# Attention and a squared-ReLU MLP on one core: the weights' sign on ScalarE, denominators on VectorE, and a new order of the work

## The chip, the cores and the metric

One core of a Trainium2 chip. The metric is the device time of one execution, in microseconds (us); smaller is better. Three runs of the kernel before took 637.91, 639.02 and 640.23 us, median 639.02.

## What is computed

q, k and v are 4 batches x 12 heads x 448 rows x 64, float32. The two weight matrices come in float64 (a float32 array times a NumPy float64 scalar), so the kernel has to turn 64-bit words into float32 itself.

```python
scores = cap * np.tanh(scale * np.matmul(q, k.transpose(0, 1, 3, 2)) / cap)
attn = np.exp(scores - np.max(scores, axis=-1, keepdims=True))
attn = attn / (np.sum(attn, axis=-1, keepdims=True) + 1e-09)
x = np.matmul(attn, v)               # 1792 tokens x 768
r = np.maximum(x @ w_in, 0.0)        # w_in 768 x 2048
out = (s * (r * r) + b) @ w_out      # w_out 2048 x 768
```

## The kernel before, in words

All work is recorded as small groups of instructions in a plan (class `Plan`). Each group has a rank, the tiles it reads and writes, and one or more engines that may do it. `emit` then runs a list scheduler over the groups: it keeps a clock per engine, takes the group that can start first (among ready ones that of the lowest rank, with a preference for the same kind of work on TensorE), books buffers, and issues the instructions in that order. Nothing is rearranged afterwards, so each engine runs its instructions strictly in the order that the scheduler's assumed times gave. The table `CHOICE` sets that order: an `at` entry (rank, step) per unit of work, the engines allowed per operation, and a few margins (`late`, `lag`, `cling`).

The units:

- `a` (batch, pair of head pairs): `load` brings K, Q and V; `scores` makes per 128 keys one TensorE product into a `ps_s` buffer (two of them), a tanh and an exp on ScalarE (L512, L516, L520). The last 64 keys of two head pairs share one chunk (the tail), which needs K and Q of both. `pv` multiplies by V and by ones into the single `ps_v` buffer in two parts (L570, L578), ScalarE copies it out (L598), and `normal` sends the sums through four small DMAs (L533), adds the two halves and the guard on GpSimd (L541, L542), takes reciprocals on VectorE (L545), and broadcasts them through DRAM (L547, L552).
- `w` (8 groups of w_in, three pieces each, `win`) and `o` (6 groups of w_out, four pieces each, `wout`): a piece is loaded as pairs of 32-bit words (`piece`, L654). In the 64-bit word the exponent has 11 bits; VectorE takes the low word down to 3 bits (L662), puts the sign in with a second pass (L663), an engine scales the high word, read as float32, by 2^-112 (L434 or L436), and VectorE shifts and joins the two (L666). For w_in the squares (L700 to L702) are summed on TensorE (the norm, L712), the largest goes through another small TensorE product that gives it to all lanes (L477), a chain of VectorE instructions of one column makes the scales (L728 to L733), and the weights are split in two float16 parts. For w_out the column sums of each group are formed by additions and one small product (L785).
- `m1` and `m2` (batch): the two MLP products, each in three float16 products (L843 to L845, L1094 to L1096). Batches 2 and 3 use a form with 7 in place of 8 block products (L1003), whose weights the units `p` prepare (`mix`).

The first two w_in groups have their pieces in the memory of `gt`, all others in a pool `w` of seven slots. All loads and stores are issued by SP, in the scheduler's order, and SP reuses eight DMA semaphores in turn.

Of the kernel before, what the change touches and what calls it, by code (L numbers as in the profile page):

```python
# [243 lines left out]
def arrange(units, at):  # L244

    key = {}
    for name, pre, _ in units:
# [5 lines left out]
    'bias': 1.806,  # L253
    'shy': {'DVE': 0.3, 'POOL': 0.5},
# [36 lines left out]
    'late': 0.621,  # L291
    'lag': 0.0,
    'cling': 19.274,
# [4 lines left out]
    'tail': 0.9,  # L298
    'evac': ('ACT',),
    'sq': ('ACT', 'DVE', 'POOL'),  # L300
    'expo': ('DVE', 'POOL'),
# [24 lines left out]
def attention_moe_kernel(  # L326
# [157 lines left out]
    def load(bb, c2, rank, vrank):  # L484
        if bb == c2 == 0:
            rank = -90
# [36 lines left out]
    def normal(bb, c2, rank):  # L523
# [15 lines left out]
        def whole():  # L539
            a = P[kc][:, 0]  # L540
            nc.gpsimd.tensor_tensor(a, a, P[kc][:, 1], ALU.add)  # L541
            nc.gpsimd.tensor_scalar(a, a, guard[:, 0:1], 0.0, ALU.add, ALU.add)  # L542

        gps(0.55, rank, whole, r=["guard", *((kc, h, i) for h in range(2) for i in range(2))], w=[kc], port=True)
        dve(0.32, rank, lambda: nc.vector.reciprocal(P[kc][:, 0], P[kc][:, 0]), w=[kc])  # L545
# [14 lines left out]
    def pv(bb, c2, rank, step):  # L560
# [54 lines left out]
        def gather():  # L615
# [6 lines left out]
            r=[("xm", bb, c) for c in range(NP)], w=[("xn", bb)], port=True,  # L622
# [24 lines left out]
    def piece(kr, src, n, rank, over=()):  # L647
# [13 lines left out]
        def sign():  # L661
            nc.vector.tensor_scalar(lo(), lo(), 29, None, ALU.logical_shift_right)  # L662
            nc.vector.scalar_tensor_tensor(lo(), hi(), -0x80000000, lo(), ALU.bitwise_and, ALU.bitwise_or)  # L663
# [508 lines left out]
    def put(name, pre, fn):  # L1172
        units.append((name, pre, fn))
# [18 lines left out]
    for d in range(ND):  # L1192
        put(("o", d), [("w", NG - 1)], lambda rank, step, d=d: wout(d, rank))
# [71 lines left out]
```

## Time and profile before

| | |
|---|---|
| median of three runs | 639.02 us |
| profiled execution | 639.61 us |
| its span (first to last instruction) | 637.8 us |
| TensorE (PE) busy | 627.0 us, 98% |
| VectorE (DVE) / ScalarE (ACT) / GpSimd (POOL) busy | 400.2 / 351.7 / 208.1 us |
| moved by DMA | 101.67 MB |

Busy TensorE time is taken from modelled ends of pipelined matmuls, so slow stretches hide in it: a matmul that runs at half the clock counts as busy. They are seen in the granted clock of a stretch and in the distance of instructions.

### The profile page before, as it was taken

To read this page: it belongs to the slowest core of one execution; us is meant where nothing else is said; L and a number is where in the kernel's file an instruction comes from. 1 tells how busy PE (TensorE), PEld (TensorE's weight loads), DVE (VectorE), ACT (ScalarE), POOL (GpSimd) and SP (SyncE) were. 2 spreads that over 40 slices of the span, in tenths; PEclk is the share of its full clock that TensorE was granted. 3 is DMA by queue.
4 is the path that set the end of the run, shared out by engine and by line. 5 is a ranking of instruction groups with operands and counts; after the bars stand their busy time and mean duration, and the time that the engine had idled before them with its cause. 6 is when DMAs were issued, how large, how long until landed. Compare 5 with 4: busy or idle time off the path is not lost.

```text
span 637.8 us, 11435 instructions
## 1 busy us (share of the span) xinstructions
PE 627.0 (98%) x4404; PEld 331.4 (52%) x4404; DVE 400.2 (63%) x810; ACT 351.7 (55%) x472; POOL 208.1 (33%) x238
## 2 busy tenths in 40 slices
PE   7999899999999999999999999999999999999997
PEld 2332344344444433434454445555558996556997
DVE  5986857888797878788773341577767222537322
ACT  5889787886884585684674531346354002445100
POOL 3343511546456544466151020117643000105000
PEclk9999899999999999999999999999999999999999
DMA  8766423654262775853854013385412774001671
GB/s 301 293 184 193 124 86 107 215 175 143 60 234 59 251 211 179 272 200 92 282 195 157 1 48 128 146 280 212 164 48 89 239 260 147 1 2 53 223 256 67
DMA packets 54774, 101.67 MB, mean 159 GB/s; under 512 B 16192, under 2 KB 34752, under 8 KB 54720
## 3 DMA queue, kind: packets, MB, share of 16 engines
q1 hardware_dynamic: 54720, 100.95, 48.2%
q8 instruction: 34, 0.56, 0.4%
q14 instruction: 20, 0.16, 0.1%
HBM read 82.58 MB, written 18.17 MB: 158 GB/s over the span
## 4 chain that ended last, share of the span: by engine, by line
PE 85%; DMA 8%; DVE 3%; ACT 1%; SPq 1%; POOL 1%; issue 0%; ACTq 0%
PE ps_v L570 9%; PE ps_m L1003 9%; PE ps_s L512 7%; PE ps_s L1003 6%; PE ps_m L843 6%; PE ps_s L844 6%; PE ps_m L844 6%; PE ps_s L843 6%; PE ps_m L845 6%; PE ps_s L845 6%; PE ps_m L1094 5%; PE ps_m L1095 5%; PE ps_m L1096 5%; PE ps_v L578 4%; DMA gt<-in_w_in 2%; DMA w<-in_w_out 2%
## 5 line engine op out<-in xcount | busy, mean ns | idle before, releaser
L1003 PEld LDWEIGHTS <-w 128*128 128x128 f16 x1008 | 96.6, 98 | 1.0
L516 ACT ACTIVATE bed<-ps_s,arena 128x896 f32<-128x896 f32 x84 | 81.5, 1006 | 9.9 <-PE ps_s L512 8.2
L520 ACT ACTIVATE bed<-bed,par 128x896 f32<-128x896 f32 x84 | 84.2, 1040 | 0.2
L570 PE MATMUL ps_v<-bed 128*32 128x448 f32 x768 | 83.0, 548 | 0.8 <-ACT pw L598 0.6
L512 PE MATMUL ps_s<-bed 64*128 64x448 f32 (+1 forms) x384 | 80.6, 578 | 1.9 <-DMA bed<-in_qT 1.6
L1094 PE MATMUL ps_m<-gt,w 128*128 128x448 f16 x192 | 67.7, 353 | 0.0
L843 PE MATMUL ps_m<-x,w 128*128 128x448 f16 x192 | 67.7, 353 | 0.0
L1096 PE MATMUL ps_m<-gt,w 128*128 128x448 f16 x192 | 67.7, 353 | 0.0
L844 PE MATMUL ps_s<-x,w 128*128 128x448 f16 x192 | 67.7, 353 | 0.0
L844 PE MATMUL ps_m<-x,w 128*128 128x448 f16 x192 | 67.7, 353 | 0.0
L845 PE MATMUL ps_m<-x,w 128*128 128x448 f16 x192 | 67.7, 353 | 0.0
L843 PE MATMUL ps_s<-x,w 128*128 128x448 f16 x192 | 67.7, 353 | 0.0
L1095 PE MATMUL ps_m<-gt,w 128*128 128x448 f16 x192 | 67.7, 352 | 0.0
L845 PE MATMUL ps_s<-x,w 128*128 128x448 f16 x192 | 67.7, 352 | 0.0
L843 PEld LDWEIGHTS <-w 128*128 128x128 f16 x384 | 37.5, 98 | 37.3 <-issue 2.1
L845 PEld LDWEIGHTS <-w 128*128 128x128 f16 x384 | 37.5, 98 | 35.0
L844 PEld LDWEIGHTS <-w 128*128 128x128 f16 x384 | 37.6, 98 | 33.8
L512 PEld LDWEIGHTS ps_s<-bed 64*128 64x128 f32 (+1 forms) x384 | 27.4, 177 | 43.5 <-issue 12.2
L938 ACT ACTIVATE pw<-ps_s,arena 128x448 f32<-128x448 f32 x32 | 20.1, 632 | 52.6 <-PE ps_s L845 49.7
L570 PEld LDWEIGHTS ps_v<-bed 128*32 128x32 f32 x768 | 20.3, 109 | 51.4 <-issue 35.7
L444 POOL TENSOR_TENSOR pw<-pw 128x224 f32<-128x224 f32 x24 | 21.6, 912 | 77.6 <-ACT pw L942 71.2
L578 PE MATMUL ps_v<-bed,ones 128*32 128x448 f32 x288 | 45.5, 545 | 0.0
(142 smaller groups left out, 1012.8 us busy)
## 6 DMA issues: line engine op xcount, KB each, us to landing
w<-w SPq DMA_DIRECT2D x48, 512.0 KB, 4.9
w<-in_w_out SPq DMA_DIRECT2D x24, 512.0 KB, 5.0
w<-ws SPq DMA_DIRECT2D x24, 512.0 KB, 4.9
w<-in_w_in SPq DMA_DIRECT2D x18, 512.0 KB, 5.5
bed<-in_v SPq DMA_DIRECT2D x24, 256.0 KB, 4.2
ws<-w SPq DMA_DIRECT2D x12, 512.0 KB, 2.9
bed<-in_kT SPq DMA_DIRECT2D x24, 224.0 KB, 3.3
bed<-in_qT SPq DMA_DIRECT2D x24, 224.0 KB, 3.6
```

Source lines behind the costliest of these rows:

```text
L512: nc.tensor.matmul(P[kp][o, h, 0:S], keys, P[q][rows], start=True, stop=True)
L516: 1.01, rank, lambda: nc.scalar.activation(P[kh], P[kp][:, :, 0:S], AF.Tanh, scale=tsc[:, 0:1]),
L520: 1.04, rank, lambda: nc.scalar.activation(P[kh], P[kh], AF.Exp, scale=par[:, 0:1]), r=["par"], w=[kh],
L570: nc.tensor.matmul(P[kp][o, 0, 0:S], P[kv][:, c, o], prob(c, h), start=(c == 0), stop=(c == NC))
L578: nc.tensor.matmul(P[kp][o, 1, 0:S], w, ph, start=first, stop=last)
L843: nc.tensor.matmul(ps[:, 0:S], wh, x[:, 0], start=(c == 0), stop=False)
L844: nc.tensor.matmul(ps[:, 0:S], wh, x[:, 1], start=False, stop=False)
L845: nc.tensor.matmul(ps[:, 0:S], wl, x[:, 0], start=False, stop=(c == NP - 1))
L1003: nc.tensor.matmul(at(), w(g, zw), b(g, zb), start=g == 0 and x == 0, stop=g == n - 1 and x == 2,)
L1094: nc.tensor.matmul(ps[:, 0:S], wh, ghi[:, f], start=(f == 0), stop=False)
L1095: nc.tensor.matmul(ps[:, 0:S], wh, glo[:, f], start=False, stop=False)
L1096: nc.tensor.matmul(ps[:, 0:S], wl, ghi[:, f], start=False, stop=(f == NF - 1))
```

## The change

Five edits, beside a new table of ranks.

1. In `piece`, the second sign pass is gone. The high word is scaled by one ScalarE instruction whose slope for negative inputs is 2^32 times that for positive ones, so that after the shift the sign stands in the right place; or, where the scheduler prefers VectorE, by two instructions. GpSimd no longer takes part.

```diff
-        def sign():
+        def low():
             nc.vector.tensor_scalar(lo(), lo(), 29, None, ALU.logical_shift_right)
-            nc.vector.scalar_tensor_tensor(lo(), hi(), -0x80000000, lo(), ALU.bitwise_and, ALU.bitwise_or)
...
-        scaled(CHOICE["expo"], n, rank, hf, hf, 2.0 ** -112, [(kr, "s")], [kr])
+        def two():
+            nc.vector.tensor_scalar(hf(), hf(), 2.0 ** -112, None, ALU.mult)
+            nc.vector.scalar_tensor_tensor(hf(), hf(), 2.0 ** 32, hf(), ALU.mult, ALU.min)
+        ways = {
+            "ACT": (
+                0.29 + n * 0.00084,
+                lambda: nc.scalar.activation(hf(), hf(), AF.Prelu, scale=2.0 ** -112, alpha=2.0 ** 32),
+            ),
+            "DVE": (0.36 + n * 0.00158, two),
+        }
```

2. In `normal`, the sum of the halves and the guard is one VectorE instruction, right before the reciprocal.

```diff
-            nc.gpsimd.tensor_tensor(a, a, P[kc][:, 1], ALU.add)
-            nc.gpsimd.tensor_scalar(a, a, guard[:, 0:1], 0.0, ALU.add, ALU.add)
+            nc.vector.scalar_tensor_tensor(a, a, guard[:, 0:1], P[kc][:, 1], ALU.add, ALU.add)
+            nc.vector.reciprocal(a, a)
```

3. In `win`, what depends on a lane's own maximum alone (`own`: root, reciprocal, square) becomes a group that may run while TensorE gives the maximum to all lanes; `fin` keeps the rest.

4. The first K, Q and cap loads get ranks far below all others (`rank = -9e12` and `-1e13` in place of -90 and -100), and `wout` may start only after all w_in groups in rank.

5. `CHOICE`: all ranks, `bias` 1.806 to 3.059, `late` 0.621 to 0.309, `lag` 0.0 to 0.452, `cling` 19.274 to 14.502, `expo` from VectorE and GpSimd to ScalarE and VectorE. For example:

```diff
-        ('w', 0): (58.5, 0.01), ('w', 1): (226.3, 0.01), ('w', 2): (-88.5, 0.01), ('w', 3): (581.8, 0.01),
+        ('w', 0): (255.1, 0.0), ('w', 1): (-84218287.2, 0.01), ('w', 2): (20.7, 0.0), ('w', 3): (256.7, 0.0),
```

How the order moves, at three places. First, SP and ScalarE at the start of the program, before the change (`bed` holds the attention tiles, `gt` and `w` the weight pieces):

```order
L1140 DMA par_130<-in_cap 128x1
L488 DMA bed_60<-in_kT 128x448
L490 DMA bed_60<-in_qT 128x448
L654 DMA w_155<-in_w_in 128x1024
L654 DMA w_157<-in_w_in 128x1024
L654 DMA w_159<-in_w_in 128x1024
L488 DMA bed_60<-in_kT 128x448
L490 DMA bed_60<-in_qT 128x448
```

```order
L1153 ACTIVATE arena_131<-par_130 128x1
L516 ACTIVATE bed_60<-ps_s_173,arena_131 128x896
L516 ACTIVATE bed_60<-ps_s_177,arena_131 128x896
L520 ACTIVATE bed_60<-bed_60,par_130 128x896 x2
L516 ACTIVATE bed_60<-ps_s_186,arena_131 128x896
```

and with it:

```order
L1156 DMA par_130<-in_cap 128x1
L488 DMA bed_60<-in_kT 128x448
L490 DMA bed_60<-in_qT 128x448
L655 DMA gt_129<-in_w_in 128x1024
L1156 DMA par_130<-in_s 128x1
L1156 DMA par_130<-in_b 128x1
L488 DMA bed_60<-in_kT 128x448 x2
L490 DMA bed_60<-in_qT 128x448 x2
```

```order
L1169 ACTIVATE arena_131<-par_130 128x1
L675 ACTIVATE gt_129<-gt_129 128x512
L516 ACTIVATE bed_60<-ps_s_173,arena_131 128x896
L516 ACTIVATE bed_60<-ps_s_180,arena_131 128x896
L520 ACTIVATE bed_60<-bed_60,par_130 128x896 x2
```

The second K and Q stand behind one weight piece in place of three, and the first tanh stands behind the scaling of that piece.

Second, SP around the sixth and last piece that goes to `gt`, before and with the change (`cmp` and `zd` belong to the denominators; the number behind `zd` is that of the head pair, counted over the batches):

```order
L547 DMA zd_2_99<-cmp_460 128x7
L547 DMA zd_3_100<-cmp_549 128x7
L494 DMA bed_60<-in_v2 128x512
L654 DMA gt_129<-in_w_in 128x1024
L552 DMA bed_60<-zd_2_99 64x448 x2
L552 DMA bed_60<-zd_3_100 64x448 x2
L533 DMA cmp_646<-pw_616 64x1x7 x3
L654 DMA gt_129<-in_w_in 128x1024
L533 DMA cmp_646<-pw_616 64x1x7
```

```order
L548 DMA zd_0_97<-cmp_301 128x7
L488 DMA bed_60<-in_kT 128x448
L490 DMA bed_60<-in_qT 128x448
L533 DMA cmp_403<-pw_372 64x1x7 x2
L553 DMA bed_60<-zd_0_97 64x448 x2
L533 DMA cmp_403<-pw_372 64x1x7 x2
L655 DMA gt_129<-in_w_in 128x1024
```

The last such load stood among the denominators of the fifth head pair (`pw_616` is its copy); it now follows those of the second.

Third, VectorE around its first TENSOR_REDUCE of a norm and the first denominators, with the change:

```order
L731 TENSOR_REDUCE arena_131<-ps_m_324 128x1
L732 TENSOR_SCALAR arena_131<-arena_131 128x1
L733 CAST brief_134<-arena_131 128x1
L541 SCALAR_TENSOR_TENSOR cmp_301<-cmp_301,arena_131 128x7
L542 RECIPROCAL cmp_301<-cmp_301 128x7
L469 TENSOR_SCALAR arena_131<-arena_131 128x1
L470 TENSOR_SCALAR arena_131<-arena_131 128x1
L471 TENSOR_SCALAR arena_131<-arena_131 128x1
L740 RECIPROCAL arena_131<-arena_131 128x1
L741 TENSOR_SCALAR arena_131<-arena_131 128x1
L663 TENSOR_SCALAR gt_129<-gt_129 128x512
L746 COPY arena_131<-ps_m_358 128x1
```

Before, VectorE had only the reciprocal of the denominators in its queue; now the sum too, which waits for four DMAs. The group L469 to L741 is `own`, and L746 begins `fin`.

Counted over the whole order: TensorE has the same matmuls, in 164 stretches of one kind in place of 159. The third norm, whose last piece is the one of the second place, stands behind nine value parts (half a head pair of `pv`, 12 matmuls) in place of thirteen: five behind the second head pair's last one, where it was three behind the fifth's. Of the first ninety ScalarE instructions, up to the ninth copy of `ps_v`, five scale weights (L675); before, in the same stretch, one was a square (L700), and there were five of the float16 parts (L433) in place of three. Of the six small products of the column sums two wait for a VectorE addition and four for a GpSimd one, as before. Of 48 weight pieces 29 are scaled on ScalarE and 19 by two instructions on VectorE; GpSimd loses 38 scalings and the 48 small instructions of the denominators. ScalarE has 485 instructions in place of 474, among them one ACT_TABLE_LOAD as before.

## Rows read from the trace of the kernel before

**Rows 1.** The page, part 1: busy us (share) of each engine.

```profile
PE 627.0 (98%) x4404; PEld 331.4 (52%) x4404; DVE 400.2 (63%) x810; ACT 351.7 (55%) x472; POOL 208.1 (33%) x238
```

**Rows 2.** TensorE's waits: engine, line, waited for: us in total, times, longest us.

```profile
PE ps_m L1163 <- POOL w L1166: 2.1, 1, 2.1
PE ps_m L712 <- DVE bed L701: 1.7, 1, 1.7
PE ps_s L512 <- DMA bed<-in_qT: 1.6, 2, 1.0
PE ps_m L785 <- DVE bed L443: 0.8, 2, 0.6
PE ps_v L570 <- ACT pw L598: 0.6, 1, 0.6
...
PE ps_m L477 <- DVE brief L722: 0.3, 1, 0.3
```

**Rows 3.** Timeline, 0 to 13 us: start, us, engine, what, count [idle before].

```profile
2.11 1.39 SPq L654 DMA_DIRECT2D w<-in_w_in  x3
...
5.10 4.12 PE L512 MATMUL ps_s<-bed 64*128 64x448 f32 x12 [0.60 <-DMA bed<-in_qT]
...
7.00 1.01 ACT L516 ACTIVATE bed<-ps_s,arena 128x896 f32<-128x896 f32 x1 [2.98 <-PE ps_s L512]
7.67 0.43 DVE L662 TENSOR_SCALAR w<-w 128x512 int32<-128x512 int32 x1 [3.43 <-DMA w<-in_w_in]
...
11.49 0.97 PE L512 MATMUL ps_s<-bed 64*64 64x448 f32 x4 [0.96 <-DMA bed<-in_qT]
```

**Rows 4.** Timeline, 66 to 69 us: the third norm and what it waits for.

```profile
66.01 1.20 POOL L702 TENSOR_TENSOR bed<-w 128x512 bf16<-128x512 f32 x1
...
66.37 1.39 DVE L666 SCALAR_TENSOR_TENSOR gt<-gt 128x512 int32<-128x512 int32 x1
...
67.79 0.69 DVE L701 TENSOR_TENSOR bed<-gt 128x512 bf16<-128x512 f32 x1
...
68.54 0.35 PE L712 MATMUL ps_m<-ones,bed 128*128 128x1 bf16 x8 [1.66 <-DVE bed L701]
```

**Rows 5.** Stretches: length, busy of each engine (x instructions), granted clock, DMA share, GB/s.

```profile
68.00:70.00 2.00, 1.46 (x20) 0.68 (x24) 1.93 (x6) 1.75 (x2) 1.90 (x3) 0.95 0.71 180
70.00:73.00 3.00, 3.00 (x19) 0.86 (x13) 1.54 (x5) 0.27 (x1) 1.25 (x2) 0.50 0.51 135
```

**Rows 6.** SP's timeline, 48 to 60 us: the last load into gt.

```profile
59.72 0.58 SPq L654 DMA_DIRECT2D gt<-in_w_in  x1
```

**Rows 7.** TensorE's timeline: a value part, two score chunks, one score chunk.

```profile
62.52 1.71 PE L570 MATMUL ps_v<-bed 128*32 128x448 f32 x16
...
64.92 1.77 PE L512 MATMUL ps_s<-bed 64*128 64x448 f32 x8
...
77.02 1.02 PE L512 MATMUL ps_s<-bed 64*128 64x448 f32 x4
```

**Rows 8.** Groups by line and shape: count | busy us, mean ns | idle before.

```profile
L663 DVE SCALAR_TENSOR_TENSOR w<-w 128x512 int32<-128x512 int32 x42 | 38.0, 906 | 1.4
...
L434 DVE TENSOR_SCALAR w<-w 128x512 f32<-128x512 f32 x8 | 3.4, 426 | 0.1
...
L700 ACT ACTIVATE bed<-w 128x512 bf16<-128x512 f32 x6 | 4.1, 688 | 1.3 <-DVE w L666 1.3
...
L436 POOL TENSOR_SCALAR w<-w 128x512 f32<-128x512 f32 x34 | 27.9, 824 | 34.9 <-DVE w L663 23.1 <-issue 2.6 <-DVE arena L728 2.5
...
L542 POOL TENSOR_SCALAR cmp<-cmp,arena 128x7 f32<-128x7 f32 x24 | 14.6, 607 | 2.4
...
L541 POOL TENSOR_TENSOR cmp<-cmp 128x7 f32<-128x7 f32 x24 | 9.9, 412 | 41.7 <-DMA cmp<-pw 33.7 <-DVE arena L470 7.9
```

**Rows 9.** Stretch of 16 us, columns as in rows 5.

```profile
48.00:64.00 16.00, 15.83 (x124) 4.47 (x124) 10.77 (x19) 15.56 (x18) 5.91 (x7) 1.00 0.69 196
```

**Rows 10.** VectorE's waits, columns as in rows 2.

```profile
DVE cmp L545 <- POOL cmp L542: 2.2, 4, 1.4
```

More of the change, by code (lines that the diff above doesn't have):

```diff
@@ L252 @@
 CHOICE = {
-    'bias': 1.806,
+    'bias': 3.059,
     'shy': {'DVE': 0.3, 'POOL': 0.5},
     'at': {
[31 rows of a table removed]
[31 rows of a table added]
     },
@@ L290 @@
     'cslag': 21,
-    'late': 0.621,
-    'lag': 0.0,
-    'cling': 19.274,
+    'late': 0.309,
+    'lag': 0.452,
+    'cling': 14.502,
     'parts': ((0, 1), (2, 3)),
@@ L298 @@
     'tail': 0.9,
+    'expo': ('ACT', 'DVE'),
     'evac': ('ACT',),
     'sq': ('ACT', 'DVE', 'POOL'),
-    'expo': ('DVE', 'POOL'),
     'whi': ('ACT', 'DVE'),
@@ L485, in load @@
         if bb == c2 == 0:
-            rank = -90
+            rank = -9e12
         kr = buf(("k", bb, c2), "kraw", [128, S], F32)
@@ L540, in whole @@
             a = P[kc][:, 0]
-            nc.gpsimd.tensor_tensor(a, a, P[kc][:, 1], ALU.add)
-            nc.gpsimd.tensor_scalar(a, a, guard[:, 0:1], 0.0, ALU.add, ALU.add)
-        gps(0.55, rank, whole, r=["guard", *((kc, h, i) for h in range(2) for i in range(2))], w=[kc], port=True)
-        dve(0.32, rank, lambda: nc.vector.reciprocal(P[kc][:, 0], P[kc][:, 0]), w=[kc])
+            nc.vector.scalar_tensor_tensor(a, a, guard[:, 0:1], P[kc][:, 1], ALU.add, ALU.add)
+            nc.vector.reciprocal(a, a)
+        dve(
+            0.38, rank, whole, r=["guard", *((kc, h, i) for h in range(2) for i in range(2))], w=[kc], port=True,
+        )
         z = zd[bb * NP + c2]
@@ L621, in pv @@
             gather,
-            r=[("xm", bb, c) for c in range(NP)], w=[("xn", bb)], port=True,
+            r=[("xm", bb, c) for c in range(NP)], w=[("xn", bb)],
         )
@@ L659, in piece @@
         hf = lambda: P[kr].bitcast(F32)[:, :, 1]
-        def sign():
+        def low():
             nc.vector.tensor_scalar(lo(), lo(), 29, None, ALU.logical_shift_right)
-            nc.vector.scalar_tensor_tensor(lo(), hi(), -0x80000000, lo(), ALU.bitwise_and, ALU.bitwise_or)
         def join():
             nc.vector.scalar_tensor_tensor(hi(), hi(), 3, lo(), ALU.logical_shift_left, ALU.bitwise_or)
-        dve(0.25 + n * 0.0018, rank, sign, r=[kr], w=[(kr, "s")], port=True)
-        scaled(CHOICE["expo"], n, rank, hf, hf, 2.0 ** -112, [(kr, "s")], [kr])
-        dve(0.07 + n * 0.0011, rank + 0.5, join, r=[kr, (kr, "s")], w=[(kr, "f")], port=True)
+        def two():
[8 more added lines that the diff above has]
+        }
+        P.any({e: ways[e] for e in engines(CHOICE["expo"])}, rank, [kr], [(kr, "h")], port=True)
+        dve(0.16 + n * 0.00052, rank, low, r=[kr], w=[(kr, "s")], port=True)
+        dve(0.07 + n * 0.0011, rank + 0.5, join, r=[kr, (kr, "s"), (kr, "h")], w=[(kr, "f")], port=True)
         return hf
@@ L725, in win, with own @@
         kl = lanes(("wps", g), rank, g, [("wnm", g)])
+        def own():
+            root2(n[:, 0:1])
+            nc.vector.reciprocal(ip[:, 0:1], n[:, 0:1])
+            nc.vector.tensor_scalar(wn[:, g:g + 1], n[:, 0:1], n[:, 0:1], None, ALU.mult)
+        dve(0.85, rank + 0.1, own, r=[("wnm", g)], w=[("wnm", g, 0)])
         def fin():
             nc.vector.tensor_copy(n[:, 1:2], P[kl][:, 0:1])
-            root2(n)
-            nc.vector.reciprocal(ip, n)
-            nc.vector.tensor_tensor(wn[:, g:g + 1], n[:, 0:1], n[:, 0:1], ALU.mult)
+            root2(n[:, 1:2])
+            nc.vector.reciprocal(ip[:, 1:2], n[:, 1:2])
             nc.vector.tensor_scalar(sw, ip[:, 1:2], 8192.0, None, ALU.mult)
             nc.vector.tensor_scalar(wc[:, g:g + 1], ip[:, 0:1], n[:, 1:2], 1.0 / 2097152.0, ALU.mult, ALU.mult)
-        dve(1.75, rank, fin, r=[kl], w=[("wnm", g), ("wc", g)], port=True)
+        dve(1.5, rank, fin, r=[kl, ("wnm", g, 0)], w=[("wnm", g), ("wc", g)])
         for c in range(NC3):
@@ L800, in wout @@
         dve(
-            0.68, rank, amax, r=[("wc", g) for g in range(NG)] + [("om", d, q) for q in range(NQ)], w=[("om", d)],
-            port=True,
+            0.68, rank, amax, r=[("wc", g) for g in range(NG)] + [("om", d, q) for q in range(NQ)], w=[("om", d)]
         )
@@ L808, in fin @@
             nc.vector.tensor_scalar(sc, wn, si, None, ALU.mult)
-        dve(1.3, rank, fin, r=[kl], w=[("op", d), ("os", d)], port=True)
+        dve(1.3, rank, fin, r=[kl], w=[("op", d), ("os", d)])
         half = NQ // 2
@@ L1139, in attention_moe_kernel @@
         dma(
-            512, -80 + i if i else -100, lambda i=i, a=a: nc.sync.dma_start(par[:, i:i + 1], a.to_broadcast([128, 1])),
+            512, -80 + i if i else -1e13, lambda i=i, a=a: nc.sync.dma_start(par[:, i:i + 1], a.to_broadcast([128, 1])),
             w=[("par", i)],
@@ L1192, in attention_moe_kernel @@
     for d in range(ND):
-        put(("o", d), [("w", NG - 1)], lambda rank, step, d=d: wout(d, rank))
+        put(("o", d), [("w", g) for g in range(NG)], lambda rank, step, d=d: wout(d, rank))
     for p in range(ND // 2):
@@ L1200, in attention_moe_kernel @@
             g = f if fast else f // 2
-            pre = [("a", j, NP - 2), ("w", g), ("w", CHOICE["alias"] - 1), *m2s]
+            pre = [("a", j, NP - 2), ("w", g), *(("w", a) for a in range(CHOICE["alias"])), *m2s]
             one = m1pair if fast else m1
```

60 rows, old and new, of the table CHOICE are left out of this document.

## The prediction

> **What bounds the kernel now.** I read the page first, then TensorE's waits, then the timeline where those waits stand, and the granted clock last. TensorE is busy 627.0 of 637.8 us [rows 1], and the change alters none of its matmuls. So nothing that is taken off VectorE (400.2), ScalarE (351.7) or GpSimd (208.1) is worth its own length; it counts only where TensorE stands still or runs slowly for it. The list of its waits is short [rows 2]: 2.1 us at the start for a GpSimd memset, 1.7 for a square of weights (L701), 1.6 for the first loads, 0.8 for column sums, 0.6 for a copy, 0.3 for a norm's maximum.
>
> One of them costs more than it shows. The third norm waits 1.66 us for VectorE at 68.54 [rows 4]. Right behind it the clock falls: 0.95 of full from 68 to 70 us and 0.50 from 70 to 73 [rows 5], which are the two levels of 2.4 and 1.2 GHz. At half the clock 3 us hold 1.5 us of work, and 0.05 x 2 = 0.1 goes before; together 1.6 us, which the busy time hides. This one place costs 1.66 + 1.6 = 3.3 us.
>
> The start is the other place. The first scores begin at 5.10, and 12 records of them take 4.12 us; the first tanh ends ScalarE's wait at 7.00; the tail chunk stands 0.96 us before 11.49 because the second Q has not landed [rows 3]. Its load was issued behind three weight pieces.
>
> **The change part by part.**
>
> *The third norm.* Before, the last piece it needs was issued at 59.72 [rows 6], the norm was due about 66.9 (68.54 less the wait), and the square that it waited for ended at 67.79 + 0.69 = 68.48 [rows 4]. So issue to square took 8.8 us and the order allowed 7.2. In the new order five value parts with their scores stand between the second head pair's last value part and the norm. A value part takes 64.92 - 62.52 = 2.40 us and two score chunks 1.77 [rows 7], 4.2 together, so five give some 21 us. The load follows that head pair's copy and denominators by a few us; even if it is issued 6 us late, 15 are left where 8.8 were needed. Moreover, the join L666 of this piece took 1.39 us while a GpSimd square ran (L702, 66.01 to 67.21) [rows 4], and GpSimd now loses 34 + 4 scalings of 0.82 us [rows 8]. I take the whole 3.3 us off. If the same wait arose again in a norm at another place, it would be nothing; the ends are -3.3 and 0, and the last is a rival below.
>
> A rule beside it: the Trainium skill (SBUF — State Buffer, "SBUF: two separate sides") says that a VectorE instruction with two SBUF inputs and a GpSimd one that reads SBUF lock each other out for the whole instruction. The 1.39 us agree with it. By that rule the new denominators' sum, with two SBUF inputs, may also stand behind a GpSimd square, and by it the sum of this prediction would be the same unless a norm stands behind that.
>
> *The start.* The second K and Q are issued behind one piece, not three. That can give back the 0.96 us of the tail chunk at most [rows 3]. Against it, the first tanh now stands on ScalarE behind the scaling of the first piece. No row has this instruction; the nearest is ScalarE's square of the same 512 columns, 0.688 us [rows 8]. Before, the first piece was there at 7.67, with two more in flight behind it [rows 3]. If it lands no sooner, the first tanh starts at 7.67 + 0.69 = 8.36, 1.36 us late, and the next scores wait for its buffer. With the two others gone it may land early enough for no delay. I set the gain and the delay against each other, 0, with ends -1.0 and +1.4.
>
> *The scaling of weights.* 29 pieces at 0.69 us are 20 us more on ScalarE. VectorE loses 48 sign passes of 0.906, and has 19 x (0.426 + 0.906) = 25 us of two-step scalings in place of ten of 0.426; GpSimd loses 38 x 0.82 [rows 8]. Most of the 20 us lies behind the attention, where ScalarE has room. In the stretch where it has little, 15.56 of 16 us from 48 to 64 [rows 9], the count is five scalings more, one square and two parts fewer: 3.4 - 0.7 - 1.4 = +1.3 us over some 75 us (a part taken at 0.69 too). Those 15.56 us are sums of instructions that follow without a gap, and TensorE was busy 15.83 then, so the room is not zero but small. I take +0.5 us, ends 0 and +1.5; what is late next is the copy L598, which frees `ps_v` and already cost 0.6 [rows 2].
>
> *Denominators.* GpSimd's 0.412 and 0.607 us per head pair [rows 8] become one small VectorE instruction. The result goes to a DMA, then to the x tiles many us ahead of their use; on TensorE it is worth 0. It moves a wait, though. GpSimd stood 33.7 us in all for these four DMAs [rows 8], and nobody cared; VectorE's queue holds joins and norms. But VectorE's reciprocal already stood at this place, and waited only 2.2 us in all, four times [rows 10]. Cost 0, ends 0 and one more stall (below).
>
> *Norms off the chain.* `own` is work that VectorE did after the broadcast product, now beside it. The wait of TensorE there, 0.3 us [rows 2], is for the maximum, which comes ahead of both; so the edit itself is worth 0 to TensorE. In the order the first norm now has a value part (2.40) between it and its broadcast where it had two chunks (1.77) [rows 7], so I take the 0.3 off; ends -0.3 and 0.
>
> *Column sums.* TensorE waited 0.8 us in two places for VectorE's last addition [rows 2]. Of the six products two still end in VectorE. I take half, -0.4; ends -0.8 and 0.
>
> *More changes of kind.* Five stretches more. Two single score chunks cost at most 2 x 1.02 = 2.04 where two in a row take 1.77 [rows 7], 0.27 us per interruption; the stretches differ in kind and some interruptions hide. I take +0.3; ends 0 and +1.4.
>
> Sum: -3.3 + 0 + 0.5 + 0 - 0.3 - 0.4 + 0.3 = -3.2 us. The profiled execution took 639.61 (span 637.8 and 1.8 around it), so 636.4 of that kind; the median of the runs shown, 639.02, is 0.6 below it. **Forecast: 635.8 us.** The good ends without the norm's (it is whole already) give -3.3 - 1.0 - 0.3 - 0.8 = -5.4, 633.6 as a median. The bad ends, with the norm still gone, give -3.3 + 1.4 + 1.5 + 1.4 = +1.0, 640.0.
>
> **The rivals.**
>
> *ScalarE takes the gain back.* It is late by 1.36 at the start and 1.3 more by the ninth copy; with no room left TensorE pays all 2.7 instead of the 0.5 that I booked, and the time is 635.8 + 2.2 = 638.0. For it speaks the 15.56 of 16 [rows 9]; against it, that TensorE's largest wait for ScalarE was 0.6 us, once [rows 2], so room was left.
>
> *VectorE held by denominators: slower.* A sum of denominators waits for its last DMA in VectorE's queue with a norm's maximum behind it, and TensorE runs dry before the broadcast. GpSimd's 33.7 us over 24 are 1.4 us each [rows 8], and the broadcast stands one value part, 2.4 us, behind its norm [rows 7]; it decides where the DMAs land over 2.4 us after VectorE came there. Each case then costs about what the third norm did, 3.3 us with the clock. One such case only puts the 3.3 back: 639.1. Two make 642.4, slower than before. Against it: 2.2 us of waits in all there [rows 10].
>
> *The start gives, and no new wait comes.* The first piece lands early, ScalarE has room: 633.6 to 634.5.
>
> *The edit is not what it says.* 19 of 48 pieces stay on VectorE at two instructions, and ScalarE might need another function table. The Trainium skill (ScalarE activation tables: per-element evaluation and per-set limits, "What a function is on this engine") has one table load between functions of two sets; the order has a single load in both kernels, so I leave no chance for that. That 19 stay is in the sums above.
>
> **How the numbers follow.** 0.3% of 639 is 1.9 us, about what a measurement here can tell: faster is below 637.1, slower above 640.9. Chances: my forecast 0.55 (634.5 to 637.5), a better start 0.13, ScalarE's rival 0.22 (637 to 639.5), VectorE's 0.10, half with one stall and half with two. Below 637.1: 0.55 x 0.9 + 0.13 + 0.22 x 0.1 = 0.65. Above 640.9: 0.05 for two stalls and 0.02 for bad ends that meet, 0.07. Between: 0.28. The range from 633.3 to 639.6 leaves out two stalls, a tenth of the good end, and the bad ends.
>
> **What would show it.** Right: no wait at the third norm and no stretch at half clock after the first 10 us; TensorE's waits in the first 80 us for ScalarE under 2 us; busy time of TensorE down by some 1.6 us through the clock alone. Wrong: a new stretch at half clock anywhere; TensorE's waits behind L516, L520 or the copy of several us, with ScalarE near 16 of 16; VectorE waiting on `cmp` DMAs ahead of a broadcast; first tanh later than 8.4.

## The result and the profile after

| | before | after |
|---|---|---|
| median of three runs | 639.02 us | 648.26 us (642.26 to 648.36) |
| ratio, 95% interval | | 1.0113 (1.008 to 1.0145) |
| profiled execution, span | 639.61, 637.8 us | 648.26, 646.5 us |

Slower by some 7 us, where 3.2 us less was forecast. Six more runs of the same kernel (`after_again`, below) had a median of 645.33 us, with a ratio of 1.009 (1.0069 to 1.0111): the second figure rests on more runs. Below, `after` is the profiled execution of 648.26 us and `after_again` the profiled one of those six (644.75 us, full clock throughout).

The page of after, part 1, answers to [rows 1]:

```profile
PE 628.2 (97%) x4404; PEld 331.4 (51%) x4404; DVE 384.1 (59%) x844; ACT 355.6 (55%) x483; POOL 174.1 (27%) x172
```

VectorE lost 16.1 us of work and GpSimd 34.0, as the edits say; ScalarE gained only 3.9 in all. TensorE's span is longer by 8.7 while its busy time rose by 1.2: it stands more. Its waits, with the columns of [rows 2]:

```profile
PE ps_s L512 <- ACT bed L516: 3.9, 4, 1.7
PE ps_m L477 <- DVE brief L733: 3.0, 2, 1.9
PE ps_v L571 <- ACT pw L599: 2.8, 3, 1.6
PE ps_m L1179 <- POOL w L1182: 2.1, 1, 2.1
PE ps_m L802 <- POOL bed L444: 1.3, 1, 1.3
PE ps_m L477 <- DVE brief L618: 0.8, 1, 0.8
PE ps_s L512 <- DMA bed<-in_qT: 0.7, 1, 0.7
PE ps_v L571 <- DMA bed<-in_v: 0.3, 1, 0.3
```

The third norm's wait (1.7 for a square, [rows 2]) is gone (its product now stands at 54.70, behind busy TensorE), and so is the wait for the second Q (0.96, [rows 3]). In their place stand eleven waits for the three other compute engines. TensorE's timeline of after at the longest ones (start, us, ..., idle before and its releaser):

```profile
12.57 1.02 PE L512 MATMUL ps_s<-bed 64*128 64x448 f32 x4 [1.67 <-ACT bed L516]
...
22.84 1.71 PE L571 MATMUL ps_v<-bed 128*32 128x448 f32 x16 [1.58 <-ACT pw L599]
...
31.82 0.16 PE L477 MATMUL ps_m<-brief,ones 128*128 128x1 bf16 x1 [1.88 <-DVE brief L733]
...
97.95 0.16 PE L477 MATMUL ps_m<-brief,ones 128*128 128x1 bf16 x1 [0.85 <-DVE brief L618]
...
109.02 0.18 PE L477 MATMUL ps_m<-brief,ones 128*128 128x1 bf16 x1 [1.12 <-DVE brief L733]
...
285.63 1.02 PE L512 MATMUL ps_s<-bed 64*128 64x448 f32 x4 [1.07 <-ACT bed L516]
287.97 0.38 PE L802 MATMUL ps_m<-arena,bed 128*128 128x1 f32 x2 [1.31 <-POOL bed L444]
```

The granted clock of the same kernel by stretches, columns as in [rows 5]:

```profile
32.00:34.00 2.00, 2.00 (x12) 0.63 (x12) 1.72 (x13) 1.01 (x1) 0.00 (x0) 0.71 0.13 10
34.00:37.00 3.00, 3.00 (x22) 0.76 (x24) 2.97 (x7) 2.25 (x3) 1.06 (x1) 0.63 0.64 152
68.00:70.00 2.00, 2.00 (x24) 0.52 (x16) 1.97 (x6) 2.00 (x4) 0.00 (x0) 1.00 0.10 19
70.00:73.00 3.00, 3.00 (x28) 1.22 (x28) 2.93 (x5) 3.00 (x5) 1.06 (x1) 1.00 0.57 154
288.00:292.00 4.00, 4.00 (x23) 1.30 (x27) 3.43 (x15) 4.00 (x7) 2.22 (x4) 0.60 0.03 5
```

From 68 to 73 us the clock is now full (0.95 and 0.50 before, [rows 5]). It falls instead behind the wait at 31.82, where (0.29 x 2 + 0.37 x 3) = 1.7 us of work are lost, and behind the two waits at 285.63 and 287.97, with 0.40 x 4 = 1.6.

What has run up by when is told by time less work: the time at which TensorE has done so many us of its matmuls, less that work at full clock. All of the difference arises in the attention and the column sums, before 295 us of work; the products behind add nothing:

```
us lost by, at TensorE's work of   31    84   113   255   295   620
before                            3.0   7.1   6.8   6.4   6.9   6.9
after                             8.0   7.1   9.7  11.1  15.3  15.3
after_again                       5.7   5.4   7.7   9.3  11.8  11.7
```

At 84 us of work, behind the third norm, `after_again` is 1.7 us ahead of before. Beside before it had lost 2.7 by the first norm and had won back more by then; it goes on to lose 2.3 around 100 us and 4.1 up to the column sums.

Waits of one order are not the same in every execution: `after_again` has 0.43 us in place of the 1.88 at 31.82, and 1.91 in place of the 0.85 at 97.95. So a wait that is there in one profile and not in another is weak evidence by itself; the times of several runs decide below.

**Where the waits come from.** The first norm of after (timeline of VectorE, GpSimd and TensorE, 26 to 32 us):

```profile
26.94 0.61 PE L723 MATMUL ps_m<-ones,bed 128*128 128x1 bf16 x12
27.10 2.48 POOL L713 TENSOR_TENSOR bed<-w 128x512 bf16<-128x512 f32 x2
...
28.70 1.17 DVE L669 TENSOR_SCALAR gt<-gt 128x512 f32<-128x512 f32 x1 [1.02 <-DMA gt<-in_w_in]
...
29.91 1.41 DVE L670 SCALAR_TENSOR_TENSOR gt<-gt 128x512 f32<-128x512 f32 x1
...
31.25 0.15 DVE L731 TENSOR_REDUCE arena<-ps_m 128x1 f32<-128x2 f32 x1
```

The norm product ended at 27.55. Its maximum (L731) stands in VectorE's queue behind the two-step scaling of a later piece, which waited 1.02 us for its load and then took 2.58 us beside GpSimd squares. So the broadcast waits 1.88 us. At 22.84 it is ScalarE's copy that comes late, with scalings ahead of it in its queue of which one waited 1.75 us for its load, at 16.10. Loads had no room in this stretch: from 8 to 28 us the 16 DMA engines were busy throughout (share 1.02 to 1.05 per 4 us, some 400 GB/s), where before the share was down to 0.77 and 0.70 from 20 to 28 us; in the first 30 us a w_in piece took a median of 8.4 us from issue to landing, against 5.1 to 6.3 before. And the fifth of the six column sums of after, behind its group's last piece, then the fourth of before:

```profile
282.36 0.44 DVE L663 TENSOR_SCALAR w<-w 128x512 int32<-128x512 int32 x1 [0.22 <-DMA w<-in_w_out]
...
283.54 3.03 POOL L444 TENSOR_TENSOR bed<-bed,w 128x512 f32<-128x512 f32 x2 [1.69 <-DVE w L666]
```

```profile
243.51 0.43 DVE L662 TENSOR_SCALAR w<-w 128x512 int32<-128x512 int32 x1 [0.49 <-DMA w<-in_w_out]
...
244.73 0.43 DVE L662 TENSOR_SCALAR w<-w 128x512 int32<-128x512 int32 x1
...
253.26 0.38 PE L785 MATMUL ps_m<-arena,bed 128*128 128x1 f32 x2
```

Before, the last piece's first pass began at 244.73 and the product came at 253.26, without a wait: the order allowed 8.5 us. After, the same pass began at 282.36 and TensorE was there at 287.97 - 1.31 = 286.66: 4.3 us allowed, 5.6 needed. Measured from a group's last landing to the start of its product, waits included, the four last column sums had 8.4 to 9.3 us before and have 5.6 to 7.3 now; the first norm 8.7 and 3.8. And the loads themselves come later along the way: the 25th of the 48 pieces landed at 137.7 us before and at 144.8 in `after_again`, the 31st at 184.4 and 203.0, the 43rd at 267.9 and 279.0.

The loss around 100 us has another source. No weight piece lands between 61.89 and 116.15 us of `after_again`; the broadcast of the first batch's x norm waits there for the denominators of that batch's last head pair:

```profile
87.77 0.23 DVE L541 SCALAR_TENSOR_TENSOR cmp<-cmp,arena 128x7 f32<-128x7 f32 x1 [3.59 <-DMA cmp<-pw]
...
95.55 0.63 DVE L443 TENSOR_TENSOR num<-pw,bed 128x448 f32<-128x448 f32 x1 [3.11 <-DMA bed<-zd]
...
97.28 0.16 PE L477 MATMUL ps_m<-brief,ones 128*128 128x1 bf16 x1 [1.91 <-DVE brief L618]
```

The sum (L541) waits for its last small DMA, the result goes through DRAM, and the product with it (L443) waits again. From the end of that head pair's copy to the broadcast the order before allowed 18.9 us and 17.5 were needed; the new one allows 15.6, and 17.4 are needed. At 109.02 of after a norm's maximum came late because VectorE, ahead of it, had waited 3.03 us for GpSimd's product with the next denominators.

### The profile page after: what moved, and what is told of

It is laid out like the page before. It is cut to its first block, busy times and chain, and to the rows that moved or that the text cites. A ratio compares the mean times of both kernels' runs of the same rounds, so it can differ in the third digit from the quotient of the medians.

```text
span 646.5 us, 11398 instructions
## 1 busy us (share of the span) xinstructions
PE 628.2 (97%) x4404; PEld 331.4 (51%) x4404; DVE 384.1 (59%) x844; ACT 355.6 (55%) x483; POOL 174.1 (27%) x172
## 4 chain that ended last, share of the span: by engine, by line
PE 78%; DMA 10%; SPq 3%; ACT 3%; DVE 3%; POOL 1%; issue 1%; DVEq 0%; POOLq 0%; ACTq 0%
PE ps_m L1019 9%; PE ps_v L571 7%; PE ps_s L1019 6%; PE ps_s L512 6%; PE ps_s L859 6%; PE ps_s L860 6%; PE ps_s L861 6%; PE ps_m L1110 5%; PE ps_m L1112 5%; PE ps_m L1111 5%; PE ps_m L859 5%; PE ps_m L860 4%; PE ps_m L861 4%; PE ps_v L579 3%; DMA gt<-in_w_in 3%; DMA w<-in_w_in 2%
## 5 line engine op out<-in xcount | busy, mean ns | idle before, releaser
L444 POOL TENSOR_TENSOR pw<-pw 128x224 f32<-128x224 f32 x20 | 17.5, 887 | 93.7 <-ACT pw L958 86.6
```

## The experiments

The texts on record number the theories as they stood when each was written: theory A and its later forms hold that the loss comes from the new order's waits; each text says what its rival is. A move runs a group of instructions directly behind a later one of its engine, and all else keeps its order; `+ A behind B` stands for that. In these lines `wr(g,i)` and `or(g,i)` are piece i of group g of w_in and w_out, `w1h(g,i)` is a float16 part of w_in; `pv(b,p)` and `pw(b,p)` are the value product of head pair p of batch b and its copy; `sc(b,p,c)` is the score product of its chunk c of keys, `ph(b,p,c)` its tanh and exp. Ratios are to runs of the kernel before on the same chip.

**Is it ScalarE's scaling?** `after_again` is the change unaltered. `tiny_slope` scales one column instead of 512, so that the instruction keeps its place and its wait but hardly any work:

```diff
-lambda: nc.scalar.activation(hf(), hf(), AF.Prelu, scale=2.0 ** -112, alpha=2.0 ** 32),
+lambda: nc.scalar.activation(hf()[:, 0:1], hf()[:, 0:1], AF.Prelu, scale=2.0 ** -112, alpha=2.0 ** 32),
```

> The changed kernel once more, nothing altered. Its three times were 648.26, 648.36 and 642.26 with granted clocks of 0.995, 0.995 and 1.000. Theory A (two places at half clock, behind TensorE's waits of 1.9 us at 32 us and 1.3 us at 288 us, make the two levels): times near 648 go with a clock of 0.995, times near 642 with 1.000, and nothing lies between but runs with one of the two falls, near 645. Rival (the times simply scatter): clock and time are not tied.

> ScalarE's 29 scalings of weights work on one column of 512, and the join shifts by 0, so that the numbers stay finite: the work of scaling is left out on ScalarE, the wait for each weight's load stays where it was in ScalarE's queue. Theory A (ScalarE stands for a load that has not landed, with tanh, exp and the copy behind it): most of the loss stays, 645 to 648. Theory B (ScalarE has 20 us more work than it has room for): about what its 20 us cost comes back, 642 or less, and TensorE's waits behind tanh and the copy are under 2 us in all.

Measured: 645.33 (1.009) and 645.15 us (1.0087, 1.0069 to 1.0106). Of `after_again`'s text half came true: its one execution with a mean clock of 0.995 took 648.45, but three with full clock took 644.06 to 645.99, not 642; two falls explain 3.4 us of the spread (half of 3.41 us each) and not all of it. The 20 us of ScalarE's new work cost nothing that shows. `no_slope` leaves the 29 ScalarE scalings out, wait and all:

> The changed kernel without ScalarE's 29 scalings: their work and their place in ScalarE's queue are both gone (19 pieces are still scaled on VectorE, and the join shifts by 0 so that the numbers stay finite). With the work alone gone and the wait for each load left in place, the time was 645.15. Theory A1 (ScalarE standing for loads, with attention behind it, is a large part of the loss): 641 to 643, and TensorE's waits behind tanh and the copy in the first 30 us and at 283 us are gone. Theory A2 (what the order asks of VectorE, GpSimd and the loads is as late, so ScalarE's waits only stand ahead of others): 644 to 645.5, and waits for the norm, the x norm and the column sums grow where ScalarE's go.

Measured: 644.7 us, 1.0093 (1.006 to 1.0126). Its TensorE waits:

```profile
PE ps_m L723 <- POOL bed L713: 2.7, 1, 2.7
PE ps_m L802 <- POOL bed L444: 2.2, 1, 2.2
```

The copy's wait went, and GpSimd's squares and column sums, which need the same late pieces, took its place. The wait for a tanh near 12.5 us stayed (1.68 at 12.38), so the scaling ahead of it was not its cause. ScalarE's scalings are not the cost by themselves.

**Are the edits themselves slow?** `before_edits` keeps the order of before and makes the first two edits alone: all 48 pieces scaled on ScalarE (none by the two VectorE instructions), no sign pass, denominators summed on VectorE.

```diff
-            nc.vector.scalar_tensor_tensor(lo(), hi(), -0x80000000, lo(), ALU.bitwise_and, ALU.bitwise_or)
...
-        scaled(CHOICE["expo"], n, rank, hf, hf, 2.0 ** -112, [(kr, "s")], [kr])
+        ... nc.scalar.activation(hf(), hf(), AF.Prelu, scale=2.0 ** -112, alpha=2.0 ** 32) ...
```

> The kernel before, its order held, with two of the edits put in place: all 48 weight pieces are scaled on ScalarE by the slope (where VectorE or GpSimd did it in the order) and have no second sign pass, and the denominators' sum is on VectorE right ahead of the reciprocal. Theory A (the order, and what stands at the head of which queue, makes the loss, not the work of the edits): 639 to 641, as the kernel before. Theory B (the edits themselves cost): 643 or more, with TensorE's waits behind tanh, exp and the copy several us longer than the 0.9 of before.

Measured: 640.08 us (12 runs) against 639.6, 1.0001 (0.9986 to 1.0016). The page, TensorE's waits, and the third norm's product:

```profile
PE 627.3 (98%) x4404; PEld 330.7 (52%) x4404; DVE 352.8 (55%) x776; ACT 377.9 (59%) x520; POOL 151.2 (24%) x152
```

```profile
PE ps_s L512 <- DMA bed<-in_qT: 1.5, 2, 1.2
PE ps_v L570 <- ACT pw L598: 1.4, 3, 0.7
PE ps_v L570 <- ACT bed L520: 1.4, 3, 0.6
PE ps_s L512 <- ACT bed L516: 0.8, 2, 0.5
...
PE ps_m L712 <- ACT bed L700: 0.5, 1, 0.5
```

```profile
70.09 0.45 PE L712 MATMUL ps_m<-ones,bed 128*128 128x1 bf16 x12
```

47 us less on VectorE, 57 less on GpSimd and 26 more on ScalarE are worth nothing in the held order. The third norm's wait of 1.7 us went by these edits alone (the 0.5 for a square is that of a later norm, at 129.20), and eight waits of at most 0.7 us for ScalarE, 3.6 in all against 0.9 (0.6 [rows 2] and 0.3 for a tanh), came in exchange. So the 1% comes with the new order, and not from these two edits as such. What the 19 two-step scalings on VectorE cost in the new order was not tested (`norm_first` below moves one of them): at 31.82 in after, and in `together` below, such a scaling stands ahead of a norm's maximum.

**What are the denominators on VectorE worth in the new order?** `sum_gpsimd` puts the sum back on GpSimd and keeps the rest of the change.

```diff
-            nc.vector.scalar_tensor_tensor(a, a, guard[:, 0:1], P[kc][:, 1], ALU.add, ALU.add)
-            nc.vector.reciprocal(a, a)
+            nc.gpsimd.tensor_tensor(a, a, P[kc][:, 1], ALU.add)
+            nc.gpsimd.tensor_scalar(a, a, guard[:, 0:1], 0.0, ALU.add, ALU.add); nc.vector.reciprocal(a, a)
```

> The changed kernel with the denominators' sum back on GpSimd, in two instructions, at the same place of the order; only the reciprocal is left on VectorE. The recorded rival (VectorE held by the sum's wait for its DMA, with norms behind): the time falls by 1 us or more, to 644 or less. Otherwise, as the order and the DMAs stay, 645 to 646.

Measured: 651.17 us, 1.0178 (1.0147 to 1.0209), 5.8 above `after_again` (5.6 by the two ratios). GpSimd's and VectorE's waits, then TensorE's:

```profile
POOL cmp L541 <- DMA cmp<-pw: 53.2, 11, 9.5
```

```profile
DVE cmp L542 <- POOL cmp L542: 29.1, 18, 5.9
```

```profile
PE ps_m L802 <- POOL bed L444: 3.0, 3, 1.3
...
PE ps_m L802 <- DVE bed L443: 1.2, 1, 1.2
```

VectorE's reciprocal waits in the same place anyway, now for DMA and GpSimd, and GpSimd's queue, with squares and column sums in it, stands too. The edit is right for this order. Since VectorE still waits there, the run does not show what the order would cost if VectorE did not wait for these DMAs.

**The tight places, one by one.** Each of these moves aims at one group of waits.

`slope_later`, three scalings later on ScalarE:

```diff
+ wr(1,0) scaling behind the tanh ph(0,0,1)
+ wr(2,2) scaling behind the tanh ph(0,1,0)
+ wr(3,1) scaling behind the copy pw(0,0)
```

> Same instructions, same engines; in ScalarE's queue three scalings stand later: the first behind two tanh, the third to need a load behind an exp and a tanh, the next behind the copy. Theory A: TensorE's waits at 12.6 (1.7 us) and 22.8 (1.6 us) go, about 3 us less than the changed kernel, 645 where that takes 648. Theory B: the same work in another order gains under 0.7 us.

Measured: 646.33 us (1.0102). The wait at 12.6 stayed (1.87 at 12.90). The copy's at 22.8 went; the norm product then waited 2.35 us at 28.23 for GpSimd's square of the piece scaled later. A miss for the gain.

`norm_first`, on VectorE:

```diff
+ wr(0,1) two-step scaling behind the first norm's maximum
```

> Same instructions; in VectorE's queue the first norm's maximum stands ahead of the two-step scaling of a weight piece instead of behind it. Theory A: the wait of 1.9 us at 31.8 goes, and with it the half clock from 33 to 36.6, which lost 1.5: 3.4 us less than the changed kernel, about 645 where that takes 648. Rival (the squares and products of the norm are late themselves, for GpSimd's sake): under 0.7 us, and the wait stays.

Measured: 645.09 us (1.0085). The wait at 31.8 went (1.88 in after, 0.43 in `after_again`); 1.74 stood at the x norm's broadcast, 96.25, as 1.91 does in `after_again`. By the times the move is worth nothing that shows.

`sums_later`, on TensorE and VectorE:

```diff
+ column sum 0 behind pv(2,4), its bias behind the next stretch
+ column sum 1 behind pv(3,3), its bias behind the next stretch
```

> The changed kernel; on TensorE two products of column sums (at 243 and 286 us) stand a score chunk and half a value part later, and on VectorE the biases behind one weight part. Theory A: their waits of 0.8 and 1.3 us go, about -2 us against the changed kernel's 645.3, 643.3. Rival (ScalarE is late at these two places as well, so TensorE waits for tanh or the copy instead): under 0.7 us.

Measured: 645.55 us (1.0089). The sums no longer waited; a tanh (1.00 at 246.69) and a copy (1.05 at 290.22) did.

`head_loads` gives the first norm's last piece its load ahead of three others, with `norm_first`:

> The changed kernel; the last piece of the group whose norm comes first is loaded ahead of three pieces of other groups, VectorE and ScalarE take the pieces in that order, and the first norm's maximum stands ahead of the next late piece. Theory A2 (the first norm's last piece, issued behind three pieces that nobody needs yet, sets the first 32 us): it lands 3.5 us sooner, near 19.5 in place of 23.2, the waits at 28 and 31 us go, and the time falls by 1.5 to 2.5 us against the changed kernel, 643 to 644. Theory A1 (ScalarE's waits at 12.6 and 22.9 set it): under 0.7 us.

Measured: 644.75 us, 1.0068 (1.0044 to 1.0092), the lowest ratio with the new order, 0.6 us below `after_again` and within its interval. The piece landed at 19.40 and the two waits went, as expected; but the loss at 31 us of work fell only from 5.7 to 4.8.

**All at once.** `all_later` joins the single moves and puts two broadcasts later; `together` moves most places at which a wait had been seen; `all_free` is `together` without ScalarE's scalings; `together2` adds the place at which `together` had stalled longest.

> The changed kernel with all the moves so far: scalings later on ScalarE, the first norm's maximum earlier on VectorE, column sums later, and the broadcasts of the first batch's x norm and of the fourth weight norm later by two score chunks and half a value part. Same work, same engines. Theory A: the time comes down to that of the kernel before or below, 638 to 641. Rival (each wait that goes is taken by the next late thing): 643 to 645.

> The changed kernel with all its work, and the places that were tight taken together: first norm's loads and maximum sooner, ScalarE's first two scalings behind tanh and exp, broadcasts of the x norm and of the fourth and sixth weight norms later on TensorE, two column sums later, a score chunk at 244 us behind half a value part, two copies ahead of what waits in front of them. The scalings that wait for loads at 280 us stay. If the losses of the places add (theory A3: the order is tight at some nine places that each cost on their own): 640 to 642. If each is only hidden behind the next (theory A4): 644 to 646.

> As the last one, and without ScalarE's 29 scalings (left out as in the run that had neither their work nor their wait). Theory A3: places at 240 to 295 us are limited by ScalarE and by the column sums side by side, so that each alone gave nothing and both give 2 to 3 us: 638 to 640, level with the kernel before. Theory A4: 643 to 645.

> As together, with the fourth broadcast's maximum (norm of group 4) ahead of five VectorE passes on two pieces of group 5 that wait for their loads, and the score chunk at 244 us back in its place. In together the first 102 us of TensorE's work lost 3.4 us less than in the changed kernel, and a wait of 2.5 us at 119.5 behind those passes, with the half clock behind it, took it back. If that queue head is what hid the gain (theory A5: VectorE stands for a weight load with a norm's maximum behind it, at a time that the loads set): that wait goes and 641.5 to 643 is measured. If another wait of the same size comes up (A4): 644.5 to 646.

Measured: 646.06 (1.011), 645.52 (1.0094, 1.0065 to 1.0122), 645.86 (1.0107) and 646.34 us (1.0119). None gained; each came out at the time of its rival or above it. In `together` the loss at 102 us of work was down to 4.3 (7.7 in `after_again`), though scores had waited 1.94 us for a tanh at 12.91, with half clock behind; then a later norm met a late load at the head of VectorE's queue:

```profile
115.86 0.43 DVE L669 TENSOR_SCALAR w<-w 128x512 f32<-128x512 f32 x1 [1.08 <-DMA w<-in_w_in]
...
119.48 0.19 PE L477 MATMUL ps_m<-brief,ones 128*128 128x1 bf16 x1 [2.52 <-DVE brief L733]
```

and the clock fell to 0.67 from 118 to 122. `together2` took those passes out of the way of the norm; the same load then held ScalarE, and a relu came 1.76 us late at 118.79 in its place:

```profile
117.53 0.70 ACT L675 ACTIVATE w<-w 128x512 f32<-128x512 f32 x1 [4.05 <-DMA w<-in_w_in]
```

**What was the third norm's stall worth?** In the kernel before, `before_norm` takes it away by order alone:

```diff
+ third norm's product behind the second part of pv(1,0)
+ its broadcast behind the scores sc(1,1,2)
```

> The kernel before with the third norm's product one value part later and its broadcast one score chunk later on TensorE, nothing else. The forecast's term: the wait of 1.7 us at 68.5 and the half clock behind it go, -3.3 us or, as the clock falls in about half of the runs, -2.5 on the median. Theory C (that stall also covered the x norm of the first batch, whose broadcast at 81.3 found its number only 1.4 us ahead): half of it comes back as a wait behind L617 at about 80, -1 to -2 us.

Measured: 638.71 us (12 runs) against 639.6, 0.9985 (0.9968 to 1.0002). Wait and half clock were gone, but a wait of 1.21 us (an exp, 76.77) was there, behind two float16 parts (L433) on ScalarE that waited 2.38 us for the norm moved. (A copy's wait of 1.00 at 63.02 lies ahead of the norm and is not of the move: `before_late` below has 1.07 there with the norm in its old place.) `before_norm2` puts these two parts behind the next exp and tanh as well:

```diff
+ w1h(1,2) behind the tanh ph(1,2,0)
+ w1h(1,1) behind the tanh ph(1,2,0)
```

> The kernel before with the third norm's product and broadcast later, as tried (638.71), and on ScalarE the two weight parts that wait for that norm's scale behind an exp and a tanh, so that TensorE does not wait at 76.8. If that wait of 1.2 us was the price of the first move: 637.5, faster than the kernel before by 0.3%. If the next late thing takes its place: 638.7.

Measured: 638.47 us (12 runs) against 640.3 (18 runs), 0.9977 (0.9961 to 0.9992): faster than both kernels, if by little. Stretches and TensorE's waits:

```profile
68.00:70.00 2.00, 2.00 (x28) 0.80 (x20) 1.74 (x3) 2.00 (x3) 1.63 (x3) 1.00 0.71 134
70.00:73.00 3.00, 2.82 (x25) 0.95 (x25) 2.79 (x15) 2.97 (x4) 1.64 (x2) 1.00 0.55 161
```

```profile
PE ps_v L570 <- DMA bed<-in_v: 1.3, 1, 1.3
...
PE ps_m L477 <- DVE brief L617: 0.6, 1, 0.6
```

The last row is the x norm of the first batch. In the kernel before its value was ready at 79.96, 1.4 us ahead of TensorE at 81.32. The stall at the third norm had covered a chain that is nearly as long.

The half clock, too, was of one execution. In the 91 executions of the kernel before that stand beside the experiments, 28 had a mean clock below 0.9985 (one such fall gives 0.997); their median was 640.97 us, that of the other 63 was 639.08.

**Late loads in the old order.** `before_late` gives the kernel before less room: the last pieces of two w_out groups are loaded later (landing at 222.14 and 247.31 in place of 218.69 and 244.71).

```diff
+ load of or(4,3) behind a denominator DMA of head pair (2,3)
+ load of or(3,3) behind a denominator DMA of head pair (2,5)
```

> The kernel before; two weight loads, the last pieces of two w_out groups, are issued later on SP, behind the small DMAs of one head pair, nothing else. Before, these pieces landed 9.25 and 8.55 us ahead of the product of their group's column sums, and TensorE waited there 0.2 and 0 us; in the changed kernel 5.6 to 7.3 us are left and it waits up to 1.3. Theory A5 (the room between the last load of a group and TensorE's product of it is what the new order took away): with some 6 us left, TensorE waits 0.5 to 2 us at each of the two, and the time is 640 to 642. Rival (6 us are enough, the waits of the changed kernel come from GpSimd's and VectorE's other work there): no wait over 0.3 us at the two, 639 to 639.5.

Measured: 640.34 us (12 runs), 1.0004 (0.9982 to 1.0027). TensorE's timeline:

```profile
228.41 0.38 PE L785 MATMUL ps_m<-arena,bed 128*128 128x1 f32 x2 [1.18 <-DVE bed L443]
...
254.72 0.38 PE L785 MATMUL ps_m<-arena,bed 128*128 128x1 f32 x2 [0.92 <-POOL bed L444]
```

The waits grew from 0.23 and 0 as the missing room says; the time did not show them. (The landing-to-product room was 6.3 and 7.4 us.) Half of the theory is borne out, the half on the total is not.

## Why the prediction was wrong

The direction was wrong, and the step that failed is the costing of the order's moves: the third norm gone for nothing, "More changes of kind" at +0.3, "Column sums" at -0.4, the first norm's -0.3, and "Denominators" at 0, with their use "many us ahead". In their place the trace of after shows eleven waits of TensorE for other engines, 11.8 us in all, where before has six with 3.7. I asked of each moved group how many instructions stand ahead of it, and took the groups I had not looked at as unchanged. I did not ask how long after its last load, or its last small DMA, each product of TensorE comes.

- *The third norm, -3.3.* The mechanism was right: from issue to the end of its square the last piece took 9.5 us (8.8 forecast), the order allowed 16.2, and wait and half clock are gone (1.7 us ahead of before at 84 us of work in `after_again`). As a term it was too large. Taken away alone it was worth 0.9 us (`before_norm`, interval down to nothing) to 1.8 (`before_norm2`; 1.5 by its ratio): new waits came at 77 and 79 us that its stall had covered, and the half clock that I booked in full comes in about a third of the executions.
- *The start, 0.* The second Q's wait went as expected, and the first tanh came at 7.87, 0.87 late, inside the ends. But the scores waited 1.67 for a tanh at 12.57, which is there without the scalings too (`no_slope`), ScalarE's next scaling waited 1.75 us for its load at 16.10, and the copy came 1.58 late at 22.84. I priced what the instruction takes (0.69 forecast, 0.690 measured over 28), not the load at the head of its queue: 29 us of such waits in all. Neither is worth time by itself (`tiny_slope`, `no_slope`).
- *First norm, -0.3.* It became 1.88 and 1.7 more by the clock in after (0.63 for a square and 0.43 for the maximum in `after_again`); the sentence on value parts counted TensorE's queue alone, and the wait is in VectorE's.
- *Column sums, -0.4.* Two waits of 0.8 in all became 1.31 and, in `after_again`, 2.1.
- *Denominators, 0.* VectorE waits 15.7 us for these DMAs, where it waited 2.2 for GpSimd [rows 10]. In this order the edit itself is worth 5.8 us (`sum_gpsimd`). But "many us ahead of their use; on TensorE it is worth 0" failed: the first batch's x norm had 1.4 us of slack before, and now TensorE waits 0.85 (`after`) to 1.91 us (`after_again`) for it behind these DMAs. The rival that went to the slower side had the wait in another place (the sum, with a norm's maximum behind it); no wait at a norm stands behind a sum in after, and the nearest, at 109.02, cost 1.12 us. `sum_gpsimd` can't rule it out as a cost, since VectorE waited there as well (29.1 us for GpSimd).
- *ScalarE takes the gain back.* Refuted for the new order, as far as the scalings go, by `tiny_slope` and `no_slope`. In the old order (`before_edits`) many small waits for ScalarE did come when the third norm's went, at a sum of zero.
- *"A new stretch at half clock anywhere"* was named as the sign of being wrong; there are two in after.

What is shown: the first two edits are free in the old order, and the new order with them costs some 6 us, in more waits for three engines and, in some executions, half clock behind them. In four experiments in which waits of the new order were taken out (`slope_later`, `sums_later`, `no_slope`, `together2`) others came; in all but `sums_later` the new one is seen behind the same late piece or its squares. That the pace of the loads sets the sum is argued from these traces and not shown, and around 100 us it is the denominators' DMAs and not the weights: `before_late` made the waits without the time, no run brought all loads of the new order forward, and none the denominators of the first batch. The cause of the whole stays open.

## What to carry to other kernels

Test an edit with the order held first; when the order is searched anew, the order is the change, and each product on the bound engine has to be asked how long after its last load or small DMA it comes, and what else stands in the queues between. An instruction that waits for a load holds everything behind it on its engine, so its price is the load's lateness and not its own length. A removed stall is worth only what is not waiting directly behind its cover: look for the next chain's slack (here 1.4 us) before booking the whole.

## What the runs showed of the chip that I had not expected

The clock does not follow the length of a wait. In the same execution it fell behind 1.88 us at 31.82, yet was 1.00 from 12 to 17 us with a wait of 1.67 at 12.57, and from 22 to 28 with 1.58 at 22.84. Other executions settle it: at the third norm it fell behind 1.66 us in the kernel before and not behind 1.70 (69.66) in `before_late`, and it stayed at 1.00 behind 1.91 (97.28) in `after_again` and 1.99 (97.83) in `sums_later`. Two stretches of after:

```profile
14.00:17.00 3.00, 2.66 (x28) 0.81 (x28) 2.97 (x7) 1.25 (x3) 0.10 (x1) 1.00 1.05 403
22.00:25.00 3.00, 2.16 (x24) 0.68 (x24) 2.44 (x7) 3.00 (x4) 0.00 (x0) 1.00 1.02 397
```

The same kernel spreads from 642.26 to 648.45 us with mean clocks of 1.000 to 0.995, in part for this reason. And a VectorE instruction with one input was stretched beside GpSimd squares too: L669 took 1.17 us at 28.70, and 0.43 at 23.20 with no square running. The Trainium skill (SBUF — State Buffer, "SBUF: two separate sides") names, beside instructions with two SBUF inputs, VectorE's two-port modes as what GpSimd locks out; no row here shows whether L669 runs in one.
